# Routing ranks moved beside attention, expert loads spread over the pairs, deeper buffers for AV and experts

## The chip, the core and the metric

The kernel runs on one core of a Trainium2 chip. The metric is the device time of one execution in microseconds. The engines are TensorE (PE; its weight loads are PEld), VectorE (DVE), ScalarE (ACT), GpSimd (POOL) and SyncE (SP); 16 DMA engines move data between HBM and SBUF. Each engine executes its own instructions in order and waits on semaphores for the others. DMAs are issued here from two queues: SP's (loads of q, k, v and writes of MoE rows) and GpSimd's (weights, gathers, scatters).

## The reference

Attention with chunk selection on 4 batches of 8 heads, 768 positions and 64 dimensions, followed by a mixture of experts on its 3072 rows of 512.

```python
k_min, k_max = k_chunks.min(3), k_chunks.max(3)      # chunks of 32 keys
ub  = sum(maximum(q * k_min, q * k_max), -1)         # bound per query and chunk, causal chunks only
sel = the 6 chunks of highest ub
scores = where(sel & causal, q @ k.T / 8, -1e9)
x = softmax(scores) @ v                              # heads side by side: [3072, 512]
y_dense = relu(x @ w1_dense) @ w2_dense
logits = x @ w_gate                                  # 8 experts
e = argmax(logits);  g = softmax(logits)[e]
out = y_dense + g * (relu(x @ w1[e]) @ w2[e])
```

## The kernel before

**Attention.** Two heads at a time make a pair: 16 pairs, four to a batch. Three loads per pair (`load`, L70) bring k, q and v as float32 through SP's queue into `aload` (3 buffers); `cast` (L280) turns them into float16 on GpSimd. `prep_k` (L288) transposes k on TensorE, takes chunk maxima and minima on VectorE and copies k into `kT`; `prep_q` (L305) transposes q and makes its positive (`qp`, ScalarE) and negative part (`qn`, VectorE); `prep_ub` (L315) computes the chunk bounds, VectorE's MAX8 finds the sixth best, and a comparison writes unselected chunks as ones beside q, so that 32 extra rows of `kT` (constants `exf`, copied by L120) push their scores down; `prep_s` (L334) transposes that. A pair then has 12 units (`PIECES`, L165). A unit is: scores on TensorE into PSUM (`scores`, L341), an exponential on ScalarE (L351), a causal mask on GpSimd for the diagonal pieces (L356), then the products with v (`av`, L360). `norm` (L380) divides by the row sums and writes the batch's rows to `xbig`. The loop (L408) issues scores two units ahead of `av`, and at set units of pair p it issues the preparation of pairs p + 1 and p + 2, the casts of pair p + 2, the loads of pair p + 3 and one expert matrix (L162).

**Fills.** When the four pairs of a batch are done, `batch_fills` (L197) makes 21 pieces of MoE work for that batch: six transposes of x, the gate (logits, argmax as one-hot columns of `ohp`, gate weight), eight pieces of the dense first layer and six of the second, whose results `ys` go to the HBM array `xd` (L257), where x itself is put too (L232). One piece is issued every second unit of the next batch's attention; they share one PSUM buffer. The last batch's pieces run after attention.

**Between.** After attention (L465 to L530) the rank of each row within its expert is computed for all 24 row tiles: matmuls with a triangular and an all-ones matrix, a scan over tiles, block starts, then slot `pos` = block and row in the block. To invert this map, `Am` (one-hot of the row in the block, 24 tiles, L515) is multiplied with `Bm` (one-hot of the block, scaled with the two digits of the row number) into `pm`, from which `gi` (rows to gather) and `si` (rows to scatter) follow.

**Experts.** 31 blocks of 128 rows (L585 on): an indirect DMA on GpSimd gathers rows of `xd` (`gather`, L539), x is transposed (`tx`), multiplied with the block's w1 (`e1`, L557, by register offset), passed through Relu, transposed back (`th`), multiplied with w2 (`e2`), and VectorE adds the dense row (`yo`, L577, which reads the gathered rows too); an indirect DMA scatters the result (L578). `xg` and `yo` have four buffers (`eg`); gathers are issued three blocks ahead.

**Order.** The program text gives the order of issue and the dependencies; the framework under it schedules each engine's instructions at build time, and moves those ahead that have nothing to wait for: the first expert load, issued in the text behind the whole preparation of pair 0, is GpSimd's first DMA in the profile.

## Time and profile before

| | |
|---|---|
| median of 2 runs | 340.62 us (339.62 to 341.62) |
| profiled execution | 341.96 us, its span 340.3 us |
| mean granted TensorE clock | 0.954 |
| busy share PE, PEld, DVE, ACT, POOL | 75%, 45%, 60%, 50%, 56% |
| DMA, mean over the span | 167 GB/s; 56.96 MB moved |
| HBM read, written | 50.08 MB, 17.66 MB |

The busy share of an engine is a mean over stages with different limits. From 28.6 to 202.6 us the trace shows attention, to 228 us the work between, and then the experts; each has to be read by itself.

### The profile page before, as it was taken

How to read it: one execution, taken by the hardware profiler on the slowest of the kernel's cores; microseconds unless marked ns; L12 is line 12 of the kernel's file. 1: busy time of each engine (PE TensorE's matmuls, PEld its weight loads, DVE VectorE, ACT ScalarE, POOL GpSimd, SP SyncE). 2: the span in 40 equal slices, each digit the busy share in tenths (PEclk: the TensorE clock that was granted, in tenths of full speed). 3: DMA queues.
4: the chain of work that ended last, by engine and by line, in shares of the span. 5: the costliest groups of instructions: out<-in, count | busy, mean ns of one | idle time of the engine just before them, and what ended most of it. 6: DMA issues, size and time to landing. Idle time of an engine off the chain costs nothing.

```text
span 340.3 us, 7383 instructions
## 1 busy us (share of the span) xinstructions
PE 253.5 (75%) x2554; PEld 152.4 (45%) x2554; DVE 205.1 (60%) x680; ACT 171.2 (50%) x319; POOL 191.3 (56%) x312
## 2 busy tenths in 40 slices
PE   0018788638889998999989979732978788777773
PEld 0005455426656566566665645411444344333331
DVE  7097889918988779987798337910333333233331
ACT  1006677717577876878768843200433333342431
POOL 2586999568545686456653330213365666557543
PEclk9999999969999999999999998975899999999997
DMA  7999999999999834512003122226165766566550
GB/s 150 264 282 214 252 218 217 214 231 232 239 271 336 253 99 117 174 64 94 2 2 127 62 94 97 94 92 187 47 206 158 231 189 203 197 211 196 184 190 4
DMA packets 60085, 56.96 MB, mean 167 GB/s; under 512 B 4302, under 2 KB 53454, under 8 KB 60048
## 3 DMA queue, kind: packets, MB, share of 16 engines
q0 software_dynamic: 14992, 28.06, 34.2%
q1 hardware_dynamic: 45056, 28.42, 29.3%
q8 instruction: 21, 0.34, 0.4%
q14 instruction: 16, 0.13, 0.1%
HBM read 50.08 MB, written 17.66 MB: 199 GB/s over the span
## 4 chain that ended last, share of the span: by engine, by line
POOL 24%; issue 22%; PE 22%; DMA 14%; DVE 10%; ACT 6%; SPq 1%; POOLq 1%; ACTq 0%; DVEq 0%
POOL out_dram L578 9%; PE yp L252 5%; POOL ex L356 5%; DMA qf<-in_q_dram 5%; DMA kf<-in_k_dram 5%; PE sp L347 4%; POOL xg L542 4%; PE hp L243 4%; ACT ex L351 4%; PE op L376 3%; DMA vf<-in_v_dram 3%; PE pp L337 2%; DVE kT L120 2%; POOL k L283 1%; DVE Am L515 1%
## 5 line engine op out<-in xcount | busy, mean ns | idle before, releaser
L351 ACT ACTIVATE ex<-sp 128x512 f16<-128x512 f32 x192 | 103.7, 617 | 47.8 <-PE sp L347 41.8
L356 POOL TENSOR_SCALAR_AFFINE_SELECT ex<-ex 128x256 f16<-128x256 f16 (+1 forms) x160 | 70.5, 453 | 46.6 <-ACT ex L351 42.3
L376 PE MATMUL op<-v,ex 128*128 128x65 f16 x768 | 57.9, 196 | 20.3 <-POOL ex L356 17.2
L347 PE MATMUL sp<-r,kT 128*128 128x512 f16 (+1 forms) x256 | 70.6, 331 | 1.1 <-ACT ex L351 0.4
L376 PEld LDWEIGHTS <-ex 128*128 128x128 f16 x768 | 41.8, 98 | 47.3 <-POOL ex L356 30.8
L551 DVE COPY exT<-tp 128x512 f16<-128x512 f16 x31 | 13.2, 425 | 71.2 <-PE tp L549 51.1
L542 POOL DMA_INDIRECT xg<-xd,gi x31 | 30.3, 976 | 44.7 <-DVE yo L577 26.1
L568 ACT COPY ehT<-tp 128x512 f16<-128x512 f16 x31 | 18.1, 585 | 43.9 <-PE tp L566 28.2
L557 PE MATMUL hp<-we,exT 128*128 x124 | 33.5, 391 | 8.2 <-issue 5.5
L578 POOL DMA_INDIRECT out_dram<-yo,si x31 | 31.5, 1015 | 13.7 <-issue 8.2
L574 PE MATMUL yp<-we,ehT 128*128 x124 | 36.2, 378 | 2.4 <-ACT ehT L568 2.3
L560 ACT ACTIVATE eh<-hp 128x512 f16<-128x512 f32 x31 | 18.5, 597 | 28.7 <-PE hp L557 26.4
L549 PE MATMUL tp<-ident,xg 128*128 128x128 f16 x124 | 12.7, 227 | 19.7 <-DMA xg<-xd,gi 19.4
L243 PE MATMUL hp<-xT,wd 128*128 128x384 f16 x128 | 26.5, 329 | 0.5
L577 DVE SCALAR_TENSOR_TENSOR yo<-yp,xg 128x512 f32<-128x512 f32 x31 | 23.2, 747 | 5.6 <-PE yp L574 3.7
L252 PE MATMUL yp<-wd,hT 128*128 128x512 f16 x96 | 26.0, 393 | 0.6 <-DVE ys L187 0.3
L328 DVE MAX8 m<-pp 128x8 f32<-128x24 f32 x192 | 18.9, 176 | 12.3 <-PE pp L322 12.2
L347 PEld LDWEIGHTS <-kT 128*128 128x128 f16 x256 | 21.9, 99 | 4.4 <-issue 1.5
L549 PEld LDWEIGHTS <-xg 128*128 128x128 f16 x124 | 7.9, 100 | 33.3 <-DMA xg<-xd,gi 30.9
L245 ACT ACTIVATE hT<-hp 128x384 f16<-128x384 f32 x32 | 15.9, 498 | 13.5 <-PE hp L243 6.8
L284 POOL CAST q<-qf 128x768 f16<-128x768 f32 x16 | 13.2, 828 | 16.2 <-DMA qf<-in_q_dram 14.1
L297 DVE TENSOR_REDUCE ks<-pp 128x8 f16<-128x256 f16 x48 | 20.0, 417 | 1.9 <-PE pp L292 1.3
(113 smaller groups left out, 414.9 us busy)
## 6 DMA issues: line engine op xcount, KB each, us to landing
we<-in_moe_w_dram POOLq DMA_DIRECT2D x16, 512.0 KB
kf<-in_k_dram SPq DMA_DIRECT2D x32, 192.0 KB, 5.0
qf<-in_q_dram SPq DMA_DIRECT2D x32, 192.0 KB, 5.4
vf<-in_v_dram SPq DMA_DIRECT2D x32, 192.0 KB, 4.9
xd<-ys SPq DMA_DIRECT2D x24, 256.0 KB, 2.1
xd<-xbig SPq DMA_DIRECT2D x8, 396.0 KB, 3.4
wd<-in_moe_w_dense_dram POOLq DMA_DIRECT2D x2, 512.0 KB
xg<-xd,gi POOLq DMA_INDIRECT x31
```

The lines of the kernel that those rows point to most:

```text
L243: nc.tensor.matmul(hp, wd[:, ko, j * 128 : (j + 1) * 128], xT[:, ko, g * G * 128 : (g + 1) * G * 128], start=(ko == 0), stop=(ko == NK - 1))
L252: nc.tensor.matmul(yp, hold["h"][:, j, i * 128 : (i + 1) * 128], wd[:, NK + j], start=(j == 0), stop=(j == NK - 1))
L347: nc.tensor.matmul(sp[:, o : o + z - a], kT[p % NB][g][:, kt * 128 : (kt + 1) * 128], s["r", g][:, a:z], start=(o == 0), stop=True, skip_g ...
L351: nc.scalar.activation(ex, sp, AF.Exp, scale=0.125)
L356: nc.gpsimd.affine_select(out=exd, in_=exd, compare_op=ALU.is_ge, fill=0.0, base=-(pc[0][0] % NJ), pattern=[[-1, n], [1, NJ], [2, 128]], c ...
L376: nc.tensor.matmul(op[:, t * (D + 1) : (t + 1) * (D + 1)], ex[:, c : c + 128], v16[p % NB][:, g, kt, :], start=(first and n == 0), stop=(l ...
L542: nc.gpsimd.indirect_dma_start(out=xg, out_offset=None, in_=xd, in_offset=bass.IndirectOffsetOnAxis(ap=gi[:, i : i + 1], axis=0))
L549: nc.tensor.transpose(tp[:, ko], s["x"][:, 2 * Dm + ko * 128 : 2 * Dm + (ko + 1) * 128].bitcast(HF), ident)
L557: nc.tensor.matmul(hp, s["xT"][:, ko], wef[:, bass.ds(offs[i] + ko * 512, 512)], start=(ko == 0), stop=(ko == NK - 1))
L574: nc.tensor.matmul(yp, s["hT"][:, j], wef[:, bass.ds(offs[i] + (NK + j) * 512, 512)], start=(j == 0), stop=(j == NK - 1))
L577: nc.vector.scalar_tensor_tensor(o, yp, s["x"][:, 3 * Dm : 3 * Dm + 2].bitcast(FP), s["x"][:, 0 : 2 * Dm].bitcast(FP), ALU.mult, ALU.add)
L578: sc = nc.gpsimd.indirect_dma_start(out=out, out_offset=bass.IndirectOffsetOnAxis(ap=si[:, i : i + 1], axis=0), in_=o, in_offset=None, bou ...
```

## The change

Loads and constants: `aload` has two buffers in place of three, and the loads of pair p + 4 are issued behind the casts of pair p + 2. Each expert matrix and the dense weights are tied behind that pair's last cast on GpSimd (`issue_after`: an order within the engine, no semaphore), one matrix in pairs 2 to 9 and two in pairs 10 to 13. `exf` is made ahead of the first cast, and its copies into `kT` go from VectorE to ScalarE. Attention: `av` runs one unit later than before (`LAG`), with six exponentials in place of five. Routing: the ranks within a batch are computed in a piece of their own (`ranks`) among the fills of the next batch, with the one-hot row digits `Am`, which now hold both digits of the row number; the last batch's run after attention. There, block numbers come from `tb` and `relb`, and `Bm` is gone: `eqb` is multiplied with the two digit planes in 48 matmuls. Experts: six buffers in place of four, and gathers four blocks ahead.

```diff
...
-    aload = att.enter_context(tc.tile_pool(name="aload", bufs=3))
+    aload = att.enter_context(tc.tile_pool(name="aload", bufs=2))
...
-    def consts():
...
+    nc.gpsimd.affine_select(out=exf, in_=exf, compare_op=ALU.is_ge, fill=0.0,
+                            base=0, pattern=pat, channel_multiplier=-32)
+    nc.gpsimd.affine_select(out=exf, in_=exf, compare_op=ALU.is_ge, fill=0.0,
+                            base=31, pattern=npat, channel_multiplier=32)
...
+            nc.vector.memset(kT[i][g][64 * g : 64 * g + 64], 0.0)
+
+    def expand(i):
+        for g in range(2):
+            nc.scalar.copy(kT[i][g][64 * g : 64 * g + 32, :], exf)
...
+    Am = const.tile([128, NM, 2, 128], HF)
...
+    def load_dense(behind):
+        with tc.issue_after(behind.ins):
+            load_dense_now()
...
+        with tc.issue_after(behind.ins):
+            nc.gpsimd.dma_start(out=we[:, e, w * NK : (w + 1) * NK], in_=src[e].rearrange("(ko ki) f -> ki ko f", ki=128))
...
+        def rank():
+
+            ohb = oh[:, b * NT : (b + 1) * NT]
+            rk = ptile("rk", [128, NT + 1, E], FP, "rk")
+            nc.tensor.matmul(rk[:, 0:NT], low, ohb, start=True, stop=False, skip_group_check=True)
+            if b:
+                nc.tensor.matmul(rk, ones, osum[:, b : b + 1].to_broadcast([128, NT + 1, E]),
+                                 start=False, stop=False, skip_group_check=True)
+            for t in range(NT):
+                nc.tensor.matmul(rk[:, t + 1 :], ones, ohb[:, t : t + 1].to_broadcast([128, NT - t, E]),
+                                 start=False, stop=t == NT - 1, skip_group_check=True)
+            rt1 = mg.tile([128, NT, E], FP, name="rt1")
+            nc.vector.tensor_tensor(rt1, rk[:, 0:NT], ohb, ALU.mult)
+            ri = mg.tile([128, NT], mybir.dt.int32, name="ri")
+            with nc.allow_low_precision("whole numbers below 2**24"):
+                nc.vector.tensor_reduce(out=ri, in_=rt1, op=ALU.add, axis=mybir.AxisListType.X)
+            r7 = mg.tile([128, NT], mybir.dt.int32, name="r7")
+            nc.vector.tensor_single_scalar(r7, ri, 127, ALU.bitwise_and)
+            rb = mg.tile([128, NT], mybir.dt.int32, name="rb")
+            nc.vector.tensor_single_scalar(rb, ri, 7, ALU.arith_shift_right)
+            rf = mg.tile([128, NT], FP, name="rf")
+            nc.vector.tensor_copy(rf, r7)
+            nc.vector.tensor_copy(relb[:, b * NT : (b + 1) * NT], rb)
+            return rk, rf
+
+        def digits(rf, t):
+            m = b * NT + t
+            nc.vector.tensor_scalar(Am[:, m, 0], io128, rf[:, t : t + 1], float(m // NJ + 1), ALU.is_equal, ALU.mult)
+            nc.vector.tensor_scalar(Am[:, m, 1], io128, rf[:, t : t + 1], iop[:, m % NJ : m % NJ + 1], ALU.is_equal, ALU.mult)
+
+        def ranks():
+            _, rf = rank()
+            for t in range(NT):
+                digits(rf, t)
+            ohb = oh[:, b * NT : (b + 1) * NT]
+            with nc.allow_low_precision("whole numbers up to 24"):
+                nc.vector.tensor_reduce(out=osum[:, b + 1], in_=ohb.rearrange("p t e -> p e t"), op=ALU.add,
+                                        axis=mybir.AxisListType.X)
+                nc.vector.tensor_add(osum[:, b + 1], osum[:, b + 1], osum[:, b])
...
+        if b + 1 < B:
+            dense.insert(4, ranks)
+        return out_list, dense, rank, digits
...
+        tc.tile_pool(name="aexp", bufs=6) as aexp,
...
+            s["cast"] = nc.gpsimd.tensor_copy(v16[p % NB][:, :, :, 0:D], s["v"])
...
+        for kind in ("tr", "h", "y", "rk"):
             cur[kind] = (pfill, "fb")
         cast(0)
-        consts()
         prep_k(0)
         prep_q(0)
+        for i in range(NB):
+            expand(i)
         prep_ub(0)
+        load(2)
+        cast(1)
+        load(3)
...
-        load(2)
-        cast(1)
...
+        def finish(p, u):
+            av(p, u)
+            if u == NU // 2 - 1:
+                norm(p, 0)
+            if u == NU - 1:
+                norm(p, 1)
+                if p % HP == HP - 1 and p + 1 < NP:
+                    a, d, _, _ = batch_fills(p // HP)
+                    fills.extend(a + d)
...
-            if u == 0:
-                if p + 3 < NP:
-                    load(p + 3)
-                if p == 1:
-                    load_dense()
-                if p == 2:
-                    route_consts()
-                if wq:
-                    load_expert(*wq.pop(0))
-                if n2 is not None:
-                    cast(n2)
...
-            av(p, u)
...
+            if i >= LAG:
+                finish(*seq[i - LAG])
+            if u == 0:
+                if n2 is not None:
+                    cast(n2)
+                    if p + 4 < NP:
+                        load(p + 4)
+                    if p == 1:
+                        load_dense(st[n2]["cast"])
+                    if p == 2:
+                        route_consts()
+                    for _ in range(2 if p >= 10 else 1):
+                        if p > 1 and wq:
+                            load_expert(*wq.pop(0), st[n2]["cast"])
+        for i in range(len(seq) - LAG, len(seq)):
+            finish(*seq[i])
+        assert not wq
...
-        tc.tile_pool(name="eg", bufs=4) as eg,
...
-
-        W = E * (NM + 1)
-        rk = p4.tile([128, 512], FP, name="rk")
-        ohf = ohp.rearrange("p e t -> p (e t)")
-        nc.tensor.matmul(rk[:, 0:W], low, ohf, start=True, stop=True, skip_group_check=True)
-        nc.tensor.matmul(rk[:, 256 : 256 + W], ones, ohf, start=False, stop=True, skip_group_check=True)
-        cs = rt.tile([128, E, NM + 1], FP)
-        nc.vector.tensor_tensor_scan(cs.rearrange("p e t -> p (e t)"), segm.rearrange("p e t -> p (e t)"),
-                                     rk[:, 256 : 256 + W], 0.0, ALU.mult, ALU.add)
+        def dense(n):
+            for _ in range(n):
+                if d:
+                    d.pop(0)()
+
+
+        dense(2)
+        rk, rf = rank()
+        cnt = rk[:, NT]
         ni = rt.tile([128, E], mybir.dt.int32)
-        nc.vector.tensor_single_scalar(ni, cs[:, :, NM], 127.0, ALU.add)
+        nc.vector.tensor_single_scalar(ni, cnt, 127.0, ALU.add)
+        digits(rf, 0)
         nc.vector.tensor_single_scalar(ni, ni, 7, ALU.arith_shift_right)
-        nb = rt.tile([128, E], FP)
...
-        nc.vector.tensor_single_scalar(ri, pos, 127, ALU.bitwise_and)
-        nc.vector.tensor_single_scalar(bi, pos, 7, ALU.arith_shift_right)
-        rf = rt.tile([128, NM], FP)
+        nc.vector.tensor_tensor(bs, be, ni, ALU.subtract)
+        digits(rf, 3)
+        tb = rt.tile([128, NM, E], FP)
+        nc.vector.tensor_tensor(tb, oh, bs.unsqueeze(1).to_broadcast([128, NM, E]), ALU.mult)
...
+        tbr = rt.tile([128, NM], FP)
+        nc.vector.tensor_reduce(out=tbr, in_=tb, op=ALU.add, axis=mybir.AxisListType.X)
+        digits(rf, 5)
...
-        Bm = rt.tile([128, NM, 2, NBLK], HF)
+        nc.vector.tensor_add(bf, tbr, relb)
         eqb = rt.tile([128, NM, NBLK], HF)
         nc.vector.tensor_tensor(eqb, ioblk.unsqueeze(1).to_broadcast([128, NM, NBLK]),
                                 bf.unsqueeze(2).to_broadcast([128, NM, NBLK]), ALU.is_equal)
-        nc.gpsimd.tensor_tensor(Bm[:, :, 0, :], eqb, iom1.unsqueeze(2).to_broadcast([128, NM, NBLK]), ALU.mult)
-        nc.vector.tensor_tensor(Bm[:, :, 1, :], eqb, iop.unsqueeze(2).to_broadcast([128, NM, NBLK]), ALU.mult)
+        dense(6)
+        pm = p4.tile([128, 2, NBLK], FP, name="pm")
+        for m in range(NM):
+            for i in range(2):
+                nc.tensor.matmul(pm[:, i], Am[:, m, i], eqb[:, m], start=(m == 0 and i == 0), stop=(m == NM - 1),
+                                 skip_group_check=True)
...
-        Am = rt.tile([128, NM, 128], HF)
-        pm = p4.tile([128, 2, NBLK], FP, name="pm")
-        for m in range(NM):
-            nc.vector.tensor_scalar(Am[:, m, :], io128, rf[:, m : m + 1], None, ALU.is_equal)
-            nc.tensor.matmul(pm, Am[:, m, :], Bm[:, m], start=(m == 0), stop=(m == NM - 1))
-            if m % 3 == 0 and d:
-                d.pop(0)()
...
+        dense(len(d))
...
+        gather(3)
         tx(0)
         for i in range(NBLK):
             e1(i)
-            if i + 3 < NBLK:
-                gather(i + 3)
+            if i + 4 < NBLK:
+                gather(i + 4)
...
```

## Rows read from the trace of the kernel before

**Rows 1.** the stretches view: busy time of each engine (instructions), clock, DMA share, GB/s.

```profile
34.00:60.00 26.00, 21.46 (x286) 14.21 (x287) 23.09 (x87) 19.15 (x38) 25.58 (x50) 1.00 1.20 229
...
120.00:150.00 30.00, 28.30 (x366) 19.03 (x364) 25.66 (x101) 21.82 (x43) 18.54 (x35) 1.00 0.39 121
...
200.00:228.00 28.00, 19.73 (x138) 10.78 (x133) 17.95 (x66) 6.51 (x14) 2.85 (x2) 0.86 0.26 96
...
245.00:330.00 85.00, 66.74 (x423) 32.20 (x420) 29.84 (x53) 31.55 (x54) 53.49 (x54) 1.00 0.63 198
```

**Rows 2.** timeline of the start: start, duration, engine, line, [idle before <-releaser].

```profile
11.80 0.83 POOL L284 CAST q<-qf 128x768 f16<-128x768 f32 x1 [6.76 <-DMA qf<-in_q_dram]
...
13.54 0.81 ACT L311 ACTIVATE qp<-pp 128x768 f16<-128x768 f16 x1 [11.45 <-PE pp L309]
...
16.89 5.38 DVE L120 COPY kT<-exf 32x768 f16<-32x768 f16 x6 [7.66 <-POOL exf L114]
...
23.10 0.56 DVE L313 TENSOR_SCALAR qn<-pp 128x768 f16<-128x768 f16 x1
...
28.59 0.60 ACT L351 ACTIVATE ex<-sp 128x512 f16<-128x512 f32 x1 [14.24 <-PE sp L347]
```

**Rows 3.** timeline near 71 us: GpSimd's cast and the AV behind it.

```profile
70.94 0.82 POOL L284 CAST q<-qf 128x768 f16<-128x768 f32 x1 [6.98 <-DMA qf<-in_q_dram]
...
73.72 0.24 PEld L376 LDWEIGHTS <-ex 128*128 128x128 f16 x4 [7.96 <-POOL ex L356]
```

**Rows 4.** one line (expert loads) and one tile (issue to landing of q loads).

```profile
L162 POOL DMA_DIRECT2D we<-in_moe_w_dram x16: 757/757/953, 1.4 to 83.0; - x16
...
DMA to landing us min/median/max: 2.6/5.4/16.4
```

**Rows 5.** timeline, VectorE's last normalisation of pairs 0, 3, 7, 11, 15.

```profile
42.36 0.55 DVE L386 TENSOR_TENSOR xbig<-op,rs 128x384 f16<-128x384 f32 x1
...
68.66 0.55 DVE L386 TENSOR_TENSOR xbig<-op,rs 128x384 f16<-128x384 f32 x1
...
119.51 0.56 DVE L386 TENSOR_TENSOR xbig<-op,rs 128x384 f16<-128x384 f32 x1
...
162.50 0.56 DVE L386 TENSOR_TENSOR xbig<-op,rs 128x384 f16<-128x384 f32 x1
...
202.05 0.56 DVE L386 TENSOR_TENSOR xbig<-op,rs 128x384 f16<-128x384 f32 x1
```

**Rows 6.** timeline between attention and experts: gather indices, first gather.

```profile
222.05 0.18 DVE L524 TENSOR_SCALAR gi<-tok 128x31 int32<-128x31 f32 x1
...
228.06 1.07 POOL L542 DMA_INDIRECT xg<-xd,gi  x1 [10.88 <-DMA xd<-ys]
```

**Rows 7.** timeline of the experts: GpSimd's gathers (L542), scatters (L578), first expert matmuls (L557).

```profile
242.48 1.03 PE L557 MATMUL hp<-we,exT 128*128 x4
...
243.48 0.95 POOL L542 DMA_INDIRECT xg<-xd,gi  x1 [10.53 <-DVE yo L577]
...
244.65 0.59 PE L557 MATMUL hp<-we,exT 128*128 x2
...
263.63 1.02 POOL L578 DMA_INDIRECT out_dram<-yo,si  x1 [0.31 <-issue]
...
264.95 0.97 POOL L542 DMA_INDIRECT xg<-xd,gi  x1 [0.30 <-issue]
...
325.58 0.97 POOL L542 DMA_INDIRECT xg<-xd,gi  x1 [1.36 <-DVE yo L577]
...
336.27 0.98 POOL L578 DMA_INDIRECT out_dram<-yo,si  x1 [1.14 <-DVE yo L577]
```

**Rows 8.** single lines: digits and kT copies, with duration min/median/max in ns.

```profile
L515 DVE TENSOR_SCALAR Am<-io,rf x24: 240/244/1428, 213.8 to 221.0; 128x128 f16<-128x128 f16 x24
...
L120 DVE COPY kT<-exf x6: 351/616/2493, 16.9 to 21.9; 32x768 f16<-32x768 f16 x6
```

**Rows 9.** the page's part 5, the masks: busy us, mean ns of one.

```profile
L356 POOL TENSOR_SCALAR_AFFINE_SELECT ex<-ex 128x256 f16<-128x256 f16 (+1 forms) x160 | 70.5, 453 | 46.6 <-ACT ex L351 42.3
```

More of the change, by code (lines that the diff above doesn't have):

```diff
@@ L104 @@
     nc.vector.memset(exf, -30000.0)
[L106 to L125 removed]
+    for g in range(2):
+        nc.gpsimd.affine_select(out=cbias[:, :, g, :], in_=cbias[:, :, g, :], compare_op=ALU.is_ge,
+                                fill=-60000.0, base=0, pattern=[[256, NT2], [1, NJ], [-32, NC]], channel_multiplier=2)
+    pat = [[256, NT2], [1, NJ], [2, 128]]
+    npat = [[-a, n] for a, n in pat]
+    nc.gpsimd.affine_select(out=exf, in_=exf, compare_op=ALU.is_ge, fill=0.0,
[3 more added lines that the diff above has]
+    for i in range(NB):
+        for g in range(2):
+            nc.vector.memset(kT[i][g][64 * g : 64 * g + 64], 0.0)
+    def expand(i):
+        for g in range(2):
+            nc.scalar.copy(kT[i][g][64 * g : 64 * g + 32, :], exf)
+    iom8 = const.tile([128, NT, E], FP)
+    oh = const.tile([128, NM, E], HF)
+    osum = const.tile([128, B, E], HF)
+    eone = const.tile([128, E], FP)
+    relb = const.tile([128, NM], FP)
+    Am = const.tile([128, NM, 2, 128], HF)
     ones = const.tile([128, 128], HF)
@@ L387, in norm @@
                                     opv[:, :, 0:D], rs.to_broadcast([128, NT, D]), ALU.mult)
-        for kind in ("tr", "h", "y"):
+        for kind in ("tr", "h", "y", "rk"):
             cur[kind] = (pfill, "fb")
         cast(0)
-        consts()
         prep_k(0)
         prep_q(0)
+        for i in range(NB):
+            expand(i)
         prep_ub(0)
+        load(2)
+        cast(1)
+        load(3)
         prep_s(0, 0)
         prep_s(0, 1)
-        load(2)
-        cast(1)
         prep_k(1)
@@ L435 @@
                 fills.pop(0)()
-            av(p, u)
-            if u == NU // 2 - 1:
-                norm(p, 0)
-            if u == NU - 1:
-                norm(p, 1)
-                if p % HP == HP - 1 and p + 1 < NP:
-                    a, d = batch_fills(p // HP)
-                    fills += a + d
-        while wq:
-            load_expert(*wq.pop(0))
+            if i >= LAG:
[15 more added lines that the diff above has]
+        assert not wq
     att.close()
@@ L453 @@
         tc.tile_pool(name="rt", bufs=1) as rt,
-        tc.tile_pool(name="eg", bufs=4) as eg,
+        tc.tile_pool(name="eg", bufs=6) as eg,
         tc.tile_pool(name="et", bufs=2) as et,
     ):
-        cur.update(tr=(p1, "tr"), h=(p2, "h"), y=(p3, "y"))
+        cur.update(tr=(p1, "tr"), h=(p2, "h"), y=(p3, "y"), rk=(p4, "rk"))
         for f in fills:
             f()
-        a, d = batch_fills(B - 1)
+        a, d, rank, digits = batch_fills(B - 1)
         for f in a:
             f()
-        W = E * (NM + 1)
@@ L488 @@
-        with nc.allow_low_precision("whole numbers below 2**24"):
-            nc.vector.tensor_reduce(out=pos, in_=c2.rearrange("p e t -> p t e"), op=ALU.add, axis=mybir.AxisListType.X)
-        ri = rt.tile([128, NM], mybir.dt.int32)
-        bi = rt.tile([128, NM], mybir.dt.int32)
-        nc.vector.tensor_single_scalar(ri, pos, 127, ALU.bitwise_and)
-        nc.vector.tensor_single_scalar(bi, pos, 7, ALU.arith_shift_right)
-        rf = rt.tile([128, NM], FP)
+        nc.vector.tensor_tensor(bs, be, ni, ALU.subtract)
```

76 lines of the change are left out of this document (23 added, 53 removed).

## The prediction, made before the change was run

> **What bounds the kernel now.** I read three stages, each from the view that names what ends last in it. First the stretches view [rows 1]. In the first four pairs of heads (34 to 60 us) GpSimd is busy 25.58 of 26 us and VectorE 23.09; the mean DMA share of 1.20 there is the highest of the four stretches. Once the fills of the MoE run beside attention (120 to 150 us) TensorE is busy 28.30 of 30 us and VectorE 25.66. Between attention and the experts (200 to 228 us) TensorE works only 19.73 of 28 us, and in the experts' stage (245 to 330 us) no engine is full: TensorE 66.74, GpSimd 53.49 of 85.
>
> Then the timeline, where these stages hand over. **Start:** the first exponential begins at 28.59 us. Its q cast waited 6.76 us for data, and VectorE then stood 7.66 us for the GpSimd constant exf and spent 5.38 us copying it [rows 2]; a first expert matrix is on the DMA engines from 1.4 us [rows 4]. **Stall:** all 16 expert matrices are issued between 1.4 and 83.0 us, and a q load takes 2.6 us to land at best, 16.4 at worst [rows 4]. One cast waited 6.98 us for such a load, and since GpSimd works in order, the masks behind it held the AV weights for 7.96 us [rows 3]. The price is read from the ends of batches: pairs 4 to 7 take 119.51 - 68.66 = 50.9 us, pairs 8 to 11 with the same work 43.0 [rows 5]. **Between:** from the last normalisation at 202.05 [rows 5] to the first gather at 228.06 is 26.0 us; the gather indices were ready at 222.05, and what the gather waited for was the last write of the dense rows [rows 6]. **Experts:** TensorE can start a block every 244.65 - 242.48 = 2.17 us while gathered rows lie ready, and GpSimd needs 0.97 + 0.30 for a gather and 1.02 + 0.31 for a scatter, 2.60 us a block, when nothing holds it [rows 7]. From the first gather to the end of the last scatter, 337.25, it took 109.2 us [rows 6, 7]; 31 x 2.60 is 80.6. The other 28.6 us GpSimd waited, mostly for a buffer that VectorE's yo still reads: four buffers, and the gather three blocks ahead needs the one of block i - 1.
>
> **The change, part by part.** Gains are negative; the sum is made on the span of 340.3 us.
>
> *Start.* The expert load at 1.4 us goes behind casts of later pairs, exf is made ahead of the first cast, and its six copies go from VectorE to ScalarE, which stood idle 14.24 us before its first exponential. Least gain: q lands as before. The cast runs from 11.80 for 0.83, and from its end to qp, which as qn needs the transposes of q, it is 0.91: qn at 13.5; qn to the first exponential stays 28.59 - 23.10 = 5.5, so 19.0, a gain of 9.6. Most: the whole 7.66 + 5.38 = 13.0. I take -12: q should land well before 11.8 without the expert's traffic, but the first cast now stands behind the constants on GpSimd. If ScalarE's copies came late (six of 768 columns, at about 0.9 us each, as 512 take 0.60), they lie inside its old idle 14.24.
>
> *First four pairs.* GpSimd loses most expert issues (0.757 us each [rows 4]). Pairs 1 to 3 take (68.66 - 42.36) / 3 = 8.8 us; VectorE alone would need 0.89 of that. So 0 to 1 us a pair, and as much again from the longer first pair: 0 to -4, taken -2.
>
> *Stall.* With one matrix a pair, issued behind that pair's cast, q, k and v arrive two pairs ahead. Six loads of 192 KB and one matrix of 512 KB per 10.7 us is 160 GB/s, two matrices (pairs 10 to 13) 210, against 229 at the full share [rows 1]. Bounds: 50.9 - 43.0 = 7.9 at most, 5 if a small wait stays; I take -7.5. Loads have two buffers in place of three, so load p + 4 waits for cast p + 2; behind it on SP's queue stand only writes whose results nothing in attention reads. GpSimd issues as many casts and matrices as before, each matrix now behind a cast that can wait for data, with the masks of the pair queued behind that cast as before.
>
> *Ranks in attention.* Per batch 12 digits at 0.244 [rows 8], and eight instructions on some 50 elements, costed no higher: 20 x 0.244 = 4.9 us of VectorE, 14.6 in three batches. VectorE is free 4.34 of 30 us [rows 1], 6.2 per 43. Nothing lost to all lost: 0 to +14.6, or more if GpSimd gets in the way (below). TensorE gets eight or nine small matmuls a batch, under 1 us. Fills are popped every second unit, and 22 still fit 24 places. I take +4.5, a third of the work, because VectorE is in order and copies and reduces queue behind a burst.
>
> Here a row speaks against the change: the same digit took 0.244 at the median and 1.428 once, and the kT copies, made while GpSimd was casting, took 0.351 to 2.493 [rows 8]. [...]
>
> *AV one unit later, six exponentials.* TensorE's idle in the fill stretch is 1.7 of 30 us [rows 1], and it can only be part of that: 0 to -4 over attention, taken -1.
>
> *Between the stages.* After the last batch the chain has fewer and narrower steps, but its result was ready 6 us before the gather [rows 6]. Only the end of the dense work counts, and that moves by what TensorE idles less while it waits for VectorE: at best -5, at worst +1 as twice as many selection matmuls (48 in place of 24) stand before the last dense pieces. I take -1.5. So the headline part is nearly free of gain.
>
> *Experts.* Six buffers, gather four ahead: the needed buffer is that of block i - 2, whose yo the scatter of block i - 2 has already waited for. From the first gather: six at 1.28 are done 7.7 us later; the first yo comes at 243.48 - 0.3 - 228.06 = 15.1, as now. Then 25 gathers and 31 scatters back to back; the last gather starts at 243.5 + 1.3 + 24 x 2.60 = 307.2 and, as now from 325.58 to 337.25, its block ends 11.7 later: 318.9 in place of 337.25, -18.3. TensorE at 2.17 keeps up; the DMA share goes from 0.63 [rows 1] to 0.63 x 3.16 / 2.60 = 0.77 (26 gathers from 243.48 to 325.58 are 3.16 apart), still under 1.20. Bounds: -3 (only the first wait shortens) and -21; I take -17, since landings will be slower with more in flight.
>
> **Sum:** -12 - 2 - 7.5 + 4.5 - 1 - 1.5 - 17 = -36.5. The profiled execution took 341.96, 1.66 around its span and 1.3 above the median of 340.62; from the median that is **304 us**.
>
> **Rivals.**
> 1. *The experts stay as they are* (13%): landings grow with more gathers in flight, and TensorE waits for them at the old pace. For it: TensorE waits for data in this stage although the buffer is what comes late. Against: GpSimd's 2.60 in the unblocked places. -3 in place of -17: 318.
> 2. *VectorE becomes the bound in attention* (12%): each of 12 digits waits one mask of 0.453 [rows 9], so 4.9 + 5.4 = 10.3 per batch against 6.2 free; 4.1 x 3 = 12.3 in place of 4.5 gives 312, and 320 if masks that wait in turn cost as much again. [...]
> 3. *The DMA stall comes back* (7%) in pairs 10 to 13, where two matrices a pair come to 210 of 229 GB/s before dense rows are written: 7 us once, 311.
> 4. *Slower* (3%): two load buffers. Should loads take longer than two pairs from issue to landing, each of the 12 casts from pair 2 on waits for the rest. 16.4 us was the worst landing under the full share, two pairs are 17.5 to 21.5. From 3.0 us a pair the gain is gone (36.5 / 12); at 4.5 it is 54 us: 358.
>
> The forecast itself has 63%; 2% is left for what I don't see. The range must take in the unknown costs: bounds that fall together on the good side give about 290, rivals 1 and 2 reach 318 to 320. So 290 to 320. Two per cent, about what a measurement of this kernel tells from no change, is 6.8 us: faster under 333.8, which only rival 4 and unseen cases miss. Faster 0.95, same 0.02, slower 0.03.
>
> **What would show it.** Start: first exponential at 15.5 to 19 us. Stall: no cast waits more than 2 us for a load, expert issues spread until pair 13, pairs 4 to 7 within 2 us of pairs 8 to 11. Ranks: batches with them at 43 to 46 us; digits over 0.4 us at the median would be rival 2. Between: the first gather still waits for dense rows, 23 to 26 us after the last normalisation. Experts: gather and scatter alternate at 2.6 us with no wait for yo after the first; a gather waiting for yo throughout, or TensorE waiting for landings at 3.1 us a block, would prove me wrong. A first exponential after 22 us, or waits for loads in every pair, would break the forecast most.

## The result and the profile after

The changed kernel takes **311.75 us** (median of 2 runs, 311.64 to 311.87) against 340.62 before: ratio 0.915, 95% interval 0.904 to 0.927. It is faster, as forecast; the forecast of 304 us was 7.75 too low, and the result lies inside its range of 290 to 320. The profiled execution has a span of 310.1 us. Ratios, here and in the table of experiments, are taken from undisturbed executions alone, and so differ by up to 0.007 from the quotients of the medians.

The stretches view of the changed kernel, with the limits laid at the ends of pairs 3, 7, 11 and 15 and at the first gather (columns as in [rows 1]):

```profile
16.20:60.20 44.00, 34.86 (x446) 23.96 (x444) 35.31 (x129) 31.78 (x60) 35.91 (x69) 0.92 0.94 203
60.20:107.10 46.90, 42.07 (x493) 27.70 (x489) 40.37 (x157) 31.04 (x62) 28.28 (x53) 0.96 0.84 196
107.10:154.00 46.90, 41.59 (x531) 28.66 (x532) 41.72 (x157) 33.52 (x66) 32.24 (x60) 1.00 0.88 195
154.00:193.40 39.40, 35.86 (x442) 23.57 (x441) 28.75 (x120) 28.44 (x57) 19.90 (x43) 0.96 0.46 96
193.40:214.00 20.60, 16.27 (x166) 9.13 (x164) 12.88 (x52) 6.18 (x13) 0.03 (x1) 1.00 0.41 155
214.00:310.10 96.10, 73.62 (x496) 37.64 (x496) 36.45 (x62) 36.58 (x62) 61.41 (x62) 0.91 0.63 195
```

The same stages in both kernels, each from the start of its first to that of its closing instruction in the timeline ([rows 2, 5, 6] for before):

| stage, us | before | after | difference | forecast |
|---|---|---|---|---|
| first exponential | 28.6 | 16.2 | -12.4 | -12 |
| pairs 0-3, from there | 40.1 | 44.0 | +3.9 | -2 |
| pairs 4-7 | 50.9 | 47.0 | -3.9 | |
| pairs 8-11 | 43.0 | 46.8 | +3.9 | |
| pairs 12-15 | 39.6 | 39.4 | -0.1 | |
| these three together | | | -0.2 | -4 |
| last normalisation to first gather | 26.0 | 20.6 | -5.4 | -1.5 |
| first gather to end | 112.2 | 96.1 | -16.1 | -17 |
| span | 340.3 | 310.1 | -30.2 | -36.5 |

**Start.** The timeline of the start (start, duration, instruction, idle before and what ended it), beside [rows 2]:

```profile
6.44 0.81 POOL L332 CAST q<-qf 128x768 f16<-128x768 f32 x1
...
9.00 4.24 ACT L121 COPY kT<-exf 32x768 f16<-32x768 f16 x5
...
10.71 0.56 DVE L361 TENSOR_SCALAR qn<-pp 128x768 f16<-128x768 f16 x1
...
16.20 0.60 ACT L399 ACTIVATE ex<-sp 128x512 f16<-128x512 f32 x1 [2.96 <-PE sp L395]
```

The q cast waits for no data, and ScalarE's copies end before its first exponential is ready. Then part of the gain is lost again. This is GpSimd's queue a little later, and TensorE's AV behind it:

```profile
16.14 0.82 POOL L334 CAST v<-vf 128x768 f16<-128x768 f32 x1
...
18.74 0.82 POOL L332 CAST q<-qf 128x768 f16<-128x768 f32 x1 [1.31 <-DMA qf<-in_q_dram]
...
20.29 1.13 POOL L404 TENSOR_SCALAR_AFFINE_SELECT ex<-ex 128x256 f16<-128x256 f16 x3
...
20.75 0.29 PE L424 MATMUL op<-v,ex 128*128 128x65 f16 x2 [3.32 <-POOL ex L404]
```

The casts run in the order of the pairs, and the one at 16.14 is the last of pair 2. So the first masks of pair 0 stand behind two casts of pair 3, which the build moved ahead, and one of which waits for its load. The masks begin 4.1 us after the first exponential; before, the first one began at 29.26, 0.7 us after it. Pair 0 takes 16.95 us instead of 13.77 (to its normalisation at 33.15).

**Ranks.** VectorE in batch 2's second pair:

```profile
128.76 0.19 DVE L376 MAX8 m<-pp 128x8 f32<-128x24 f32 x1
...
129.82 0.18 DVE L376 MAX8 m<-pp 128x8 f32<-128x24 f32 x1
...
130.16 0.23 DVE L268 TENSOR_SCALAR Am<-io,rf 128x128 f16<-128x128 f16 x1
130.31 0.30 DVE L269 TENSOR_SCALAR Am<-io,rf,iop 128x128 f16<-128x128 f16 x1
...
132.73 0.39 DVE L269 TENSOR_SCALAR Am<-io,rf,iop 128x128 f16<-128x128 f16 x1
133.04 0.89 DVE L376 MAX8 m<-pp 128x8 f32<-128x24 f32 x9
133.88 0.52 DVE L378 TENSOR_TENSOR q<-pp,m 128x144 f16<-128x144 f32 x2
```

Three of the twelve maxima of the next pair are out, then come all twelve digits, then the other nine. TensorE's matmuls for these maxima had ended by 128.73; the transposes that need q (L385) began at 134.25, after TensorE had idled 2.21 us for them. The longer pieces of the chain of waits are all VectorE's from 118.99 to 134.25.

**Stall.** It is gone: the longest wait of a cast for a load is the 1.31 us above (6.98 in [rows 3]), q loads land in 2.3 to 7.4 us, and the expert loads are issued from 39.2 to 163.2 us (L168).

**Experts.** GpSimd's timeline in the middle and at the end of the stage:

```profile
242.31 0.97 POOL L589 DMA_INDIRECT xg<-xd,gi  x1 [0.30 <-issue]
243.58 1.02 POOL L625 DMA_INDIRECT out_dram<-yo,si  x1 [0.30 <-DVE yo L624]
244.90 0.97 POOL L589 DMA_INDIRECT xg<-xd,gi  x1 [0.30 <-issue]
...
294.22 0.97 POOL L589 DMA_INDIRECT xg<-xd,gi  x1 [0.30 <-issue]
```

A gather and a scatter follow each other every 2.59 us without a gap, as the forecast had it; the last gather starts 80.3 us after the first one (213.97).

### The profile page after: what moved, and what is told of

It reads as the page before. It is cut to its first block, busy times and chain, and to the rows that moved or that the text cites. A ratio compares the mean times of both kernels' runs of the same rounds, so it can differ in the third digit from the quotient of the medians.

```text
span 310.1 us, 7557 instructions
## 1 busy us (share of the span) xinstructions
PE 249.7 (81%) x2607; PEld 154.7 (50%) x2607; DVE 207.9 (67%) x720; ACT 174.6 (56%) x325; POOL 188.4 (61%) x309
## 3 DMA queue, kind: packets, MB, share of 16 engines
q0 software_dynamic: 14992, 28.06, 40.1%
## 4 chain that ended last, share of the span: by engine, by line
PE 30%; POOL 19%; issue 17%; DVE 12%; DMA 8%; ACT 7%; SPq 4%; POOLq 1%; ACTq 0%; DVEq 0%
DMA xg<-xd,gi 6%; ACT ex L399 6%; PE sp L395 5%; POOL ex L404 5%; PE yp L298 5%; POOL xg L589 5%; PE op L424 4%; PE hp L289 4%; SPq L76 4%; POOL out_dram L625 3%; PE hp L604 3%; DVE Am L269 2%; PE pp L385 2%; DVE m L376 2%; POOL v L334 2%
## 5 line engine op out<-in xcount | busy, mean ns | idle before, releaser
L399 ACT ACTIVATE ex<-sp 128x512 f16<-128x512 f32 x192 | 101.5, 618 | 27.8 <-PE sp L395 24.5
L395 PE MATMUL sp<-r,kT 128*128 128x512 f16 (+1 forms) x256 | 71.8, 336 | 5.3 <-ACT ex L399 3.9
L424 PEld LDWEIGHTS <-ex 128*128 128x128 f16 x768 | 44.4, 100 | 36.0 <-POOL ex L404 17.5
L625 POOL DMA_INDIRECT out_dram<-yo,si x31 | 31.4, 1014 | 22.6 <-DVE yo L624 17.1
L624 DVE SCALAR_TENSOR_TENSOR yo<-yp,xg 128x512 f32<-128x512 f32 x31 | 23.3, 751 | 15.6 <-PE yp L621 15.6
L621 PE MATMUL yp<-we,ehT 128*128 x124 | 31.8, 379 | 0.9 <-ACT ehT L615 0.8
L395 PEld LDWEIGHTS <-kT 128*128 128x128 f16 x256 | 22.9, 100 | 6.7 <-issue 3.0
L376 DVE MAX8 m<-pp 128x8 f32<-128x24 f32 x192 | 19.6, 174 | 8.2 <-PE pp L370 7.9
L387 DVE COPY r<-pp 128x768 f16<-128x768 f16 x32 | 17.1, 551 | 8.4 <-PE pp L385 8.4
L596 PEld LDWEIGHTS <-xg 128*128 128x128 f16 x124 | 8.3, 101 | 28.9 <-DMA xg<-xd,gi 26.7
L385 PE MATMUL pp<-ident,q 128*128 128x128 f16 x192 | 15.0, 225 | 7.5 <-DVE q L378 7.4
```

What stands on the lines that cost most here:

```text
L376: nc.vector.max(out=m8[:, t, g], in_=ub[:, t, g])
L395: nc.tensor.matmul(sp[:, o : o + z - a], kT[p % NB][g][:, kt * 128 : (kt + 1) * 128], s["r", g][:, a:z], start=(o == 0), stop=True, skip_g ...
L399: nc.scalar.activation(ex, sp, AF.Exp, scale=0.125)
L424: nc.tensor.matmul(op[:, t * (D + 1) : (t + 1) * (D + 1)], ex[:, c : c + 128], v16[p % NB][:, g, kt, :], start=(first and n == 0), stop=(l ...
L621: nc.tensor.matmul(yp, s["hT"][:, j], wef[:, bass.ds(offs[i] + (NK + j) * 512, 512)], start=(j == 0), stop=(j == NK - 1))
L624: nc.vector.scalar_tensor_tensor(o, yp, s["x"][:, 3 * Dm : 3 * Dm + 2].bitcast(FP), s["x"][:, 0 : 2 * Dm].bitcast(FP), ALU.mult, ALU.add)
```

## The experiments

There were three series of four kernels, each beside new runs of the kernel before, whose medians were 346.4, 340.2 and 346.3 us. The first two series ran on one chip, the third on another. One thing must be known to read them: in the first and third series the experts' stage ran 16 to 22 us slower in all kernels with six buffers than in the second, for a cause that stays open (last section), so totals of different series are not compared; the stages ahead of the first gather repeat within 2 us and are compared. In the first series the kernel before scattered from 342.3 to 352.2 us, and the totals of its four kernels (the first four rows) are too uncertain for a verdict; the argument rests on the stages.

| us | pairs 0-3 | 4-7 | 8-11 | 12-15 | to gather | experts | time | ratio, 95% |
|---|---|---|---|---|---|---|---|---|
| ranks after attention | 43.2 | 42.4 | 41.8 | 38.0 | 25.6 | 114.4 | 323.46 | 0.937 (0.926-0.949) |
| no lag | 44.5 | 48.4 | 45.4 | 42.2 | 19.9 | 117.6 | 333.10 | 0.963 (0.950-0.976) |
| four buffers | 43.3 | 46.7 | 48.4 | 39.5 | 20.6 | 115.2 | 330.40 | 0.956 (0.937-0.975) |
| loads not tied | 52.1 | 55.4 | 47.6 | 38.4 | 20.6 | 114.8 | 344.39 | 1.001 (0.995-1.008) |
| changed kernel | 43.9 | 47.0 | 46.9 | 39.4 | 20.6 | 96.3 | 309.60 | 0.910 (0.905-0.916) |
| digits spread | 43.1 | 44.0 | 43.4 | 35.9 | 20.6 | 95.7 | **300.89** | **0.887** (0.881-0.894) |
| cast later | 43.1 | 45.5 | 48.2 | 38.0 | 20.6 | 96.2 | 310.51 | 0.916 (0.909-0.922) |
| four buffers again | 43.3 | 46.7 | 48.4 | 39.5 | 20.6 | 109.2 | 325.18 | 0.956 (0.949-0.962) |
| ranks after, again | 45.1 | 42.4 | 41.8 | 38.0 | 25.6 | 114.5 | 325.29 | 0.942 (0.936-0.949) |
| not tied, again | 51.4 | 55.2 | 47.6 | 38.4 | 20.6 | 112.2 | 343.48 | 0.994 (0.988-1.001) |
| spread, cast later | 44.1 | 44.1 | 43.4 | 35.9 | 20.6 | 112.8 | 318.65 | 0.925 (0.917-0.932) |
| spread, no lag | 43.9 | 45.4 | 45.2 | 38.8 | 19.9 | 115.0 | 325.44 | 0.940 (0.933-0.947) |

### Ranks after attention

```
...
-            dense.insert(4, ranks)
+            late.append(ranks)
...
+        for f in late:
+            f()
```

> The changed kernel with the ranks and digits of batches 0 to 2 computed after attention, behind the first two dense pieces of the last batch, instead of among the fills. Theory (the ranks' burst on VectorE holds the next pair's chunk maxima, and is what pairs 4 to 7 and 8 to 11 lose): these two batches fall from 47.0 and 46.8 us to 43 to 44 each, pairs 12 to 15 stay at 39 to 40, and the stretch between attention and the first gather grows from 20.6 by what three rank chains cost on VectorE there, 4 to 10 us; in all 308 to 315 us. Rival (the later AV or the weights' traffic made these batches long): they stay at 46 to 47, and with the longer stretch the whole takes 316 to 322.

Pairs 4 to 15 take 122.2 us in place of 133.2, and the tail (from the last normalisation to the first gather) 25.6 in place of 20.6: the ranks cost 11.0 us in attention and save 5.0 behind it. The total missed the expected 308 to 315 us by the experts' 114.4, which the edit didn't touch. In the later run of the same kernel, no digit stands between the copies of k and the maxima, and all twelve go out together:

```profile
124.56 1.16 DVE L377 MAX8 m<-pp 128x8 f32<-128x24 f32 x12
```

In the tail of that run TensorE waits for VectorE, with the last dense pieces queued behind the selection; the third line is the same piece of work in the changed kernel:

```profile
199.74 1.44 PE L560 MATMUL pm<-eqb,Am 128*128 128x31 f16 x48 [3.66 <-DVE eqb L554]
201.02 3.84 PE L299 MATMUL yp<-wd,hT 128*128 128x512 f16 x12
...
207.53 2.88 PE L298 MATMUL yp<-wd,hT 128*128 128x512 f16 x12
```

The twelve dense matmuls take 3.84 us in place of 2.88. After the wait TensorE's granted clock is 0.5 from 199.8 to 203.3 us (mean over the tail 0.93), where the changed kernel has 1.00 throughout this stage, so 1.0 of the 5.0 us is the clock's.

The 11.0 is the whole price of the ranks in that place. It doesn't yet tell a burst in the way of the maxima from a VectorE that is simply full.

### Digits spread over the dense pieces

```
...
-            dense.insert(4, ranks)
...
+            for t in range(NT):
+                dense[2 + 2 * t] = with_digits(dense[2 + 2 * t], t)
+            dense.insert(2, first)
```

> The changed kernel, unaltered, as the yardstick of the three kernels that run beside it. In its first profile its stages took: first exponential at 16.2 us, pairs 0-3 44.0 us, pairs 4-7 47.0, 8-11 46.8, 12-15 39.4, last norm to first gather 20.6, experts 96.1, span 310.1. Kernels that left the experts' code as it is took 114 to 118 us for the experts on another chip. If the chip makes that difference, this run shows either 96 or 114 us in the experts and repeats every other stage within 1 us; if one of those edits made it, this run shows 96 us wherever it is run.

> The ranks of a batch stay in the next batch's attention, but the digits are issued two at a time (one block's pair, 0.55 us) behind six pieces of the dense work, not twelve in one burst of 3.3 us. Theory (the burst stands in VectorE's order ahead of the maxima of the next pair, and the pair waits for it): pairs 4-7 and 8-11 take 43 to 44.5 us each in place of 47, pairs 12-15 38 to 39, the end of attention comes 6 to 8 us earlier, the tail and the experts stay as in the changed kernel, span some 304. Rival (VectorE is full in this stretch, 41 of 47 us, and any 5 us more are paid wherever they stand): 47 and 47 us as before the edit, within 1 us, span 310.

These are the same instructions, so the same work on VectorE, but one block's two digits stand behind every second dense piece, and the ranks without digits (`first`) two places earlier:

```profile
124.30 0.19 DVE L388 MAX8 m<-pp 128x8 f32<-128x24 f32 x1
124.41 0.23 DVE L268 TENSOR_SCALAR Am<-io,rf 128x128 f16<-128x128 f16 x1
124.56 0.31 DVE L269 TENSOR_SCALAR Am<-io,rf,iop 128x128 f16<-128x128 f16 x1
124.78 1.08 DVE L388 MAX8 m<-pp 128x8 f32<-128x24 f32 x11
```

One block's digits now stand among the maxima, not six. The three batches take 44.0, 43.4 and 35.9 us, 9.9 less than in the changed kernel beside it, which repeated its first profile within 0.3 us stage by stage. Of the 11.0 only 1.1 is left. TensorE's weight loads for the transposes of q wait 1.1 us in all for VectorE from pair 4 on, in the changed kernel 6.9. The rival, a VectorE that is full, is refuted: the same work now fills a larger share of VectorE's time, and the batches are shorter, as the stretches of pairs 4 to 7 and 8 to 11 show:

```profile
59.03:103.07 44.04, 40.59 (x510) 27.31 (x506) 41.34 (x157) 32.39 (x63) 28.91 (x54) 1.00 0.91 217
103.07:146.42 43.35, 41.21 (x522) 28.05 (x520) 41.06 (x157) 33.23 (x65) 31.20 (x59) 1.00 0.93 202
```

At 300.89 us (0.887 of the kernel before) this is the fastest version that ran, 0.972 of the changed kernel beside it. The edit does two things, as the ranks also start two places earlier; that part wasn't run alone. The unaltered kernel's run gave 96.3 us for the experts; its expectation speaks of another chip, but the kernels of the first series had run on the same one.

### Loads not tied to the casts

```
...
-        with tc.issue_after(behind.ins):
-            load_dense_now()
+        load_dense_now()
...
-        with tc.issue_after(behind.ins):
-            nc.gpsimd.dma_start(out=we[...], ...)
+        nc.gpsimd.dma_start(out=we[...], ...)
```

> The changed kernel with the dense and expert weights not tied behind casts, so that the build puts them on GpSimd's queue as early as it can, most of them within the first four or five pairs. Theory (the traffic of the weights made the casts wait): a cast waits 4 to 8 us for a q or k load around pair 3 or 4, the first eight pairs end 4 to 9 us later than 107.1, in all 315 to 321. Rival (two load buffers and the new place of cast and load keep the loads early whatever the weights do): no wait over 2 us, in all 310 to 313.

> The kernel whose weight loads are not tied to the casts once more, for the same reason as the run beside it: its experts took 114.8 us in the first series. If the chip made that, the experts take 95 to 98 us, pairs 0-3 take 52 us and pairs 4-7 55 us again, and the span is 326 us, so that the tie alone is worth some 16 us. If the edit made it, the experts take 114 us and the span is 344.

The stall is back, and doubled: pairs 0 to 3 lose 8 us and pairs 4 to 7 as much. The chain of waits in the second run (start, length, what ended last) holds two loads that take 35.7 us of it between 27.58 and 81.02:

```profile
27.58 18.93 DMA qf<-in_q_dram
46.63 0.83 POOL q L330
47.45 0.37 POOL ex L402
...
64.11 16.77 DMA kf<-in_k_dram
81.02 0.54 POOL k L329
```

Casts wait 4.6 and 7.6 us for these, with masks behind them. Around the end of each wait TensorE's granted clock falls to 0.5, from 44.8 to 51.7 and from 79.0 to 89.2 us (means: 0.88 from 16 to 60 us, 0.83 from 60 to 90), as it did once at the stall of the kernel before (0.51 from 70.2 to 77.1), so the price of a stall holds the time at the lower clock too. The expert loads are all issued between 22.1 and 84.8 us. The tie is worth 15.3 us here (pairs 0 to 15: 192.5 us in the second run against 177.2), twice the 7.5 forecast for the stall. The theory of the first run was too small: the first eight pairs were to end 4 to 9 us later and ended 16 later. So the tie removes more than the old stall. That the start, 12 us earlier, and the two load buffers let the early pairs meet the weights as well is argued; neither was run apart.

### No lag

```
...
-        LAG = 1
+        LAG = 0
...
```

> The changed kernel with AV issued in its old place (lag 0), six exponentials kept. Theory (the lag is nearly free; ranks make the batches long): pairs 4 to 7 and 8 to 11 within 1 us of 47.0 and 46.8, in all 311 to 314. Rival (the lag moves the normalisations and the order behind them, and costs the 4 us a batch): these batches at 43 to 44, in all 303 to 307.

> Digits spread over six pieces, but each AV matmul group issued in its own unit, not one unit later. With the digits in one burst, taking the lag away cost 3.6 us in pairs 0-15 (135.9 to 139.5 less the start). If the lag covers the wait of TensorE for the masks of a unit, taking it away costs 3 to 6 us here too: span 302 to 305. If the lag only covered what the burst of digits held up, it costs nothing once they are spread: span 298 to 299.5.

Without the lag, pairs 0 to 15 take 3.3 us more with the burst of digits in place, and 6.8 more once it is spread; the tail gives 0.7 back in both. The first run met neither of its expectations, as the three batches moved by +1.4, -1.5 and +2.8 us. What AV waits for from pair 4 to the end of attention (engine, waiting line, what ended the wait: us in total, times, longest), with the lag in the changed kernel and then without it:

```profile
PEld L424 <- POOL ex L404: 6.8, 18, 0.8
PE op L424 <- POOL ex L404: 2.7, 10, 0.4
```

```profile
PEld L424 <- POOL ex L404: 15.5, 34, 0.9
PE op L424 <- POOL ex L404: 6.6, 22, 0.7
```

The lag does cover waits for masks. It is worth more where VectorE's burst doesn't hold the pair up anyway.

### The cast later

```
...
-            if u == 0:
+            if u == (4 if p == 0 else 0):
                 if n2 is not None:
                     cast(n2)
...
```

> The casts of pair 2 (and the load of pair 4 behind them) are issued behind the masks of the first five units of pair 0, not behind the first one. Theory (GpSimd waits for the load of pair 2 with the masks of pair 0 queued behind it): pair 0 takes 14 us from the first exponential in place of 17, pairs 0-3 41 us in place of 44, span 3 us shorter. Rival (pairs 0-3 are held by GpSimd's whole work there, casts, masks and constants, or by the loads' own pace): pair 0 gets faster but pairs 1 and 2 give it back, pairs 0-3 stay 43.5 to 44.5 us, span within 1 us.

> Digits spread over six pieces, and in pair 0 the casts of pair 2 issued behind the fifth unit's masks. Each edit alone: the first took 11 us from the span, the second 2.6 (pair 0 16.1 us in place of 16.9, the rest scattered over the batches). If they add, the span is 296 us, with pairs 0-3 at 43 us. If the second only moved norms within VectorE's order, it gives nothing here and the span is 298 to 300 us.

This says nothing on its theory, because the edit moved other casts than those in the way. It names the casts of pair 2 (the first two lines below); the build still puts them ahead of the masks of pair 0, and they begin before the first exponential at 15.76 us, as in the changed kernel. The casts ahead of the masks are those of pair 3, which the program issues in pair 1:

```profile
12.87 0.83 POOL L331 CAST k<-kf 128x768 f16<-128x768 f32 x1 [0.57 <-DMA kf<-in_k_dram]
...
15.71 0.82 POOL L334 CAST v<-vf 128x768 f16<-128x768 f32 x1
...
18.30 0.82 POOL L332 CAST q<-qf 128x768 f16<-128x768 f32 x1 [1.29 <-DMA qf<-in_q_dram]
19.06 0.83 POOL L331 CAST k<-kf 128x768 f16<-128x768 f32 x1
19.84 1.13 POOL L404 TENSOR_SCALAR_AFFINE_SELECT ex<-ex 128x256 f16<-128x256 f16 x3
```

Pair 0 took 16.1 us here, but 16.1 also with the digits spread and 17.1 with both edits. In the first two of these runs TensorE's clock goes with the time. After its wait for the first masks, score matmuls of 512 columns take 0.62 us in place of 0.38; the last of that length starts at 22.35 us here (mean clock of pair 0: 0.89) and at 25.45 in the changed kernel (0.80; pair 0: 16.95). With the digits spread the mean over pairs 0 to 3 is 0.96, in the changed kernel 0.92. The run with both edits doesn't fit: its exponentials of pair 0 keep the changed kernel's times within 0.1 us, and its page shows a clock of at least 0.9 in every slice there. The edit itself gives nothing (310.51 against 309.60).

### Four buffers

```
...
-        tc.tile_pool(name="eg", bufs=6) as eg,
+        tc.tile_pool(name="eg", bufs=4) as eg,
...
-            if i + 4 < NBLK:
-                gather(i + 4)
+            if i + 3 < NBLK:
+                gather(i + 3)
...
```

> The changed kernel with the experts as before: four buffers, gathers three blocks ahead. Theory (GpSimd's wait for a buffer that yo still reads set the pace): gathers wait for yo again, 3.1 to 3.2 us a block, the stage from the first gather to the end grows from 96.1 to 111 to 113, in all 326 to 329. Rival (the pace came from elsewhere, as less other traffic or the better placed gathers): under 3 us a block, in all 312 to 318.

> Four buffers for gathered rows and for results, gathers issued three blocks ahead, as in the kernel before; all else as in the changed kernel. Theory (the sixth buffer lets GpSimd issue a gather and a scatter of every block back to back, 2.6 us per block): the experts take 112 us in place of 96 on a chip where the changed kernel takes 96, span 16 us longer, all other stages within 1 us. Rival (the experts' pace is set by something else, such as the rate of the transfers on the chip, and the buffers give little): within 2 us of the changed kernel beside it.

In the series where the changed kernel's experts took 96.3 us, four buffers took 109.2. GpSimd's gathers wait for yo again:

```profile
245.69 0.97 POOL L589 DMA_INDIRECT xg<-xd,gi  x1 [0.75 <-DVE yo L624]
...
248.42 0.97 POOL L589 DMA_INDIRECT xg<-xd,gi  x1 [0.44 <-DVE yo L624]
```

Over the run 23 gathers wait 27.5 us in all for yo; in the changed kernel none does. The buffers are worth 12.9 us of the stage and 15.6 of the time (325.18 to 309.60), of which 1.5 arises in pairs 8 to 11, in both runs of this kernel, for a cause that I don't know. But in the first series four buffers took 115.2 us and the three kernels with six 114.4 to 117.6: there they seem to be worth nothing, though no kernel of that series differs from this one by the buffers alone.

### Ranks after attention, again

This is no new edit, but the kernel of the first series beside others.

> The kernel with all ranks behind attention once more, beside others this time, to settle its experts' stage of 114 us. The changed kernel and the kernel with spread digits took 96 us there on the same chip in the series before this one. If something on the chip made the first figure, the experts take 95 to 98 us here, the rest repeats (pairs 4-15 122 us, tail 25.6), and the span is 303 us, between the kernel with spread digits (298.6) and the changed one (310.0). If the edit makes it (other work in attention shifts what the experts wait for), the experts take 114 us again and the span is 321.

The experts take 114.5 us again, which by itself would speak for the edit. But the kernel with spread digits and a later cast, beside it, takes 112.8, and it differs from the one that took 95.7 only in where the program issues the casts of pair 2, and in the chip; and the same four-buffer kernel took 115.2 and 109.2 us on one chip. So this edit alone can't be the cause, and the chip alone isn't either: one chip showed both paces.

## Why the prediction came out as it did

**Start: right**, -12.4 against -12, with the first exponential, the q cast and the copies where the forecast put them. No run took the start's edits back, so what each of them gives isn't shown.

**First four pairs: wrong sign**, +3.9 against -2. I counted expert issues that leave GpSimd and not what the earlier start does: pair 0 now begins while the loads of pair 3 are still coming, the casts that wait for them stand ahead of its masks, and 3.2 of the 3.9 us are lost in that pair. The clock has a part in it. TensorE stood 3.32 us for those masks, and its granted clock is 0.5 from 19.9 to 26.7 us; the kernel before has 1.00 all through pair 0. The stretches view of pair 0 alone, before and then after (the clock is the third column from the end):

```profile
28.60:42.40 13.80, 10.83 (x132) 6.77 (x131) 11.12 (x39) 10.79 (x21) 13.43 (x34) 1.00 1.20 238
...
16.20:33.20 17.00, 12.38 (x130) 8.28 (x129) 11.02 (x39) 11.22 (x20) 12.15 (x24) 0.80 0.83 194
```

With some 3.4 us at that clock in place of 6.8 (digits spread, the cast later; worked out from the means of 0.96 and 0.89) pair 0 takes 16.1 us, 0.8 less; in proportion the clock has 1.7 of the 3.2 us, which is an estimate from these runs, and the run with both edits doesn't bear it out. That the casts are the cause of the wait is read from the trace; the experiment meant to show it moved other casts.

**Stall: right in kind.** No cast waits over 2 us, and pairs 4 to 7 take as long as 8 to 11 (47.0 and 46.8). Taking the tie away brings back 15.3 us, more than there was before. Of the -0.2 us of the three batches, ranks are +11.0 and the lag -2.7 (no lag against the changed kernel), which leaves -8.5 for the stall, against -7.5. That is a remainder, if the parts add: it also holds the sixth exponential and the two load buffers, which weren't run alone.

**Ranks in attention: the step that failed.** It was the 4.5, "a third of the work": 11.0 us were measured. VectorE's free time was counted as if the work could fall into it. The twelve digits are ready at one moment and go out in one burst, ahead of nine maxima on which the next pair's scores hang, so nearly all of it is on the path; spread, it costs 1.1. The second rival gave 12.3 for this, by another mechanism: digits that each wait for a whole mask of GpSimd. No run shows it for the digits as a whole: their medians stay at 0.244 and 0.314 us (L268, L269), while single ones take up to 0.485 and 0.712; with the ranks after attention, where GpSimd is idle, none is over 0.25 and 0.31. By the means (0.270 and 0.371 against 0.247 and 0.308) that is 2.1 us over all 48. Spread over the dense pieces the digits reach 0.710 and 0.856 us, and the price is 1.1 all the same. So that rival's price was close by luck, and its mechanism isn't what costs the 11.0.

**AV one unit later: too small.** I took -1; the runs without the lag show -2.6, and -6.1 with the digits spread (tail included). I had bounded it at -4 by TensorE's idle in the kernel before, and the kernel with spread digits breaks that bound.

**Between the stages: mis-sized**, -5.4 against -1.5. I saw that the last dense rows end this stage, and held the ranks to be out of its way. They are in it: the selection matmuls wait for VectorE's digits, and twelve dense matmuls are queued behind them. With the ranks back in the tail TensorE waits 3.66 us there and 5.0 us return, 1.0 of them by the lower clock after the wait; VectorE is then busy 19.43 of 25.5 us, in the changed kernel 12.88 of 20.6.

**Experts: right in mechanism, the size with a caution**, -16.1 against -17; the sum had the last gather at +79.1 us from the first, and it came at +80.3. But it isn't sure that both profiles had the same pace (last section). The profile of before lacks landing times like the slower ones, and three of its gathers come over 4 us after the one ahead of them, once the first scatter is out; six do in the slow profile with four buffers and none in the quick one. The time of that kernel, 340.62 us, is that of the quick series (340.2) and not of the slow ones. Between kernels of the quick series the buffers gave -12.9, so that the closeness of 16.1 to 17 may in part be luck. Landings are a little later with more in flight, as I had assumed for the 17: in the quick profiles gathers land in 4.2 to 4.6 us at the median with six buffers, in 3.9 with four. The first rival (experts as they are) fell for the run that was forecast, but describes the series in which six buffers took 112 to 118 us. The changed kernel itself never ran at that pace.

**Two load buffers (the slower rival):** it didn't come. The casts don't wait for loads in every pair; in the changed kernel the loads of q, k and v land within 9.8 us, against two pairs of 17.5.

The sum -36.5 became -30.2. The ranks gave 6.5 us less than forecast, the first pairs 5.9 and the experts 0.9; the tail gave 3.9 more, the lag in the three batches 1.7, the stall 1.0 and the start 0.4. That is 13.3 - 7.0 = 6.3, so the total came closer than its parts by luck. Most of the rest of the 7.75 is that the profiled execution before was 1.3 us above its median. Two signs named in advance failed with the parts: batches of 47.0 and 46.8 us against 43 to 46, and 20.6 us between the stages against 23 to 26.

## What to carry to other kernels

Work moved under an in-order engine's slack is priced by what stands behind it at the moment when it becomes ready, not by the engine's busy share: issue it in pieces the size of the gaps (here 11.0 us in one burst, 1.1 spread). A stage that ends with one engine's output is shortened also by freeing another engine if the first one's queue has a wait on it in the middle (here by 5.0 us). An earlier start meets the loads of the next pairs earlier too, and here lost part of its gain at casts that waited for them (3.2 of 12.4 us in pair 0). After a long wait look at TensorE's granted clock: in pair 0 and at the stalls, work at 0.5 of the clock came on top of the wait (6.8 us of it behind a wait of 3.32 in pair 0).

## What was not expected of the hardware

The experts' stage has two paces for the same instructions. In the five profiles with the quick one (the changed kernel twice, digits spread, cast later: 96 us; four buffers: 109) the profile gives a time from issue to landing for GpSimd's transfers (4.2 us for gathers in the changed kernel). In the other nine, that of the kernel before among them, it gives none, for the expert loads in attention neither, since the trace holds only part of these landings, and the stage takes 112 to 118 us. The lines view of the steady part, in the quick kernel with spread digits and then in the slow one with the later cast (busy, mean ns, idle before and what ended it):

```profile
L637 POOL DMA_INDIRECT out_dram<-yo,si x28 | 28.5, 1016 | 18.1 <-DVE yo L636 12.9 <-issue 4.3 <-DVE exT L610 0.9
...
L627 ACT COPY ehT<-tp 128x512 f16<-128x512 f16 x28 | 16.4, 585 | 30.0 <-PE tp L625 30.0
```

```profile
L616 PE MATMUL hp<-we,exT 128*128 x110 | 30.8, 405 | 11.2 <-issue 9.6 <-DVE exT L610 1.6
...
L637 POOL DMA_INDIRECT out_dram<-yo,si x27 | 27.5, 1018 | 34.4 <-DVE yo L636 29.0 <-issue 5.4
...
L627 ACT COPY ehT<-tp 128x512 f16<-128x512 f16 x28 | 16.4, 586 | 44.7 <-remote 18.9 <-PE tp L625 17.3 <-PE yp L633 4.5
```

No instruction is longer on GpSimd or ScalarE; TensorE, VectorE and ScalarE pause together, ScalarE for up to 3.8 us, on releases that the profile can't name. TensorE's granted clock falls to 0.5 at some of these pauses, as from 237.9 to 241.3 us (0.7 in that slice of the page, 0.86 over the stage), which makes its matmuls longer (four of `yp` take 1.58 us there and 1.03 at 242.93; 405 ns at the mean, 379 in the quick kernel). But the two profiles with four buffers have mean granted clocks of 0.956 and 0.954 and differ by 6.0 us in this stage, so the clock alone isn't the cause. Within each of the three series all kernels had the same pace. What sets it stays open; whether a deeper ring of buffers would cover it wasn't tried.
